# Two blocks of 512 rows as one unit in a two-level Strassen MLP, with six row tiles normalised earlier

## The chip, the cores and the metric

One NeuronCore of a Trainium2 chip runs the whole kernel. The metric is the device time of one execution in microseconds (us). TensorE (PE) does the matmuls, its weight loads are shown as PEld; VectorE is DVE, ScalarE is ACT, GpSimd is POOL, and SyncE (SP) issues the transfers between DRAM and SBUF. All data are FP32.

## The reference

Attention with random features (8 batches, 8 heads, 576 positions, 64 channels, 128 features), then a Fourier mix over positions and channels with a residual, then a normalised two-layer MLP of 512 to 2048 to 512 over 8 x 576 = 4608 rows:

```python
q_p, k_p = phi(q * scale), phi(k * scale)   # phi: exp(x omega^T - |x|^2/2 - max) / sqrt(m)
kv, z = einsum('bhsm,bhsd->bhmd', k_p, v), sum(k_p, axis=2)
x = einsum('bhsm,bhmd->bhsd', q_p, kv) / (einsum('bhsm,bhm->bhs', q_p, z)[..., None] + 1e-06)
...
u = x + real(fft(fft(x, axis=1), axis=2))    # x as (8, 576, 512)
un = (u - mean(u)) / sqrt(var(u) + 1e-06)
out = u + maximum(un @ w_ch1, 0.0) @ w_ch2
```

## The kernel before, in words

**Two parts.** The first part (up to about 423 us in the profile) does the attention of 32 pairs of heads, the Fourier mix (its sums u go to a DRAM tensor `us`), the conversion of the weights, and the MLP of the first 512 rows in four plain tiles of 128 rows. The second part does the MLP of the other 4096 rows in eight blocks of 512 rows (`TB`, `NTB` = 8, numbered j = 0 to 7).

**How a block is computed.** Both layers use Strassen's scheme in Winograd's form (seven products in place of eight), twice nested: a layer is seven outer products (i), each of seven inner ones (n), so 49 "leaves". The order of outer products is `ORDER1` in the first layer and `order(j)` in the second; that of the inner ones is `PARTS` (L1210). A leaf of the first layer (`first_of`, L1495) is four matmuls of 128x128 by 128 rows into one PSUM bank; a leaf of the second (`product_of`, L1892) accumulates four such matmuls into 128 columns. Block 0 does six of its first-layer outer products with one level only (L1646; matmuls of 128 by 256 columns), as the weight sums for two levels are not ready then.

**The operands.** The first layer's weights stay in SBUF (`w1`), with outer sums in `so` (5, 6 and 3), the inner sums of product 1 in `w1s`, and other inner sums in DRAM (`w1l`, three for each of six products, written in block 0 by `w1_inner`). Each block from 1 on loads those 18 (`wx`, L1789, 256 KB each), and every block loads the 49 leaves of the second layer from `w2l` (`wl`, L1798, 256 KB each). Both share one ring of 12 buffers (`wl`, `NWL`). The hidden rows lie in `hid`, four outer cells C11, C12, C21, C22 with four inner cells (f, t) each. The left sums of the second layer (`left_sums`, and `sums` in `product_of`) are added by DVE or POOL (`add`, L1460), as the planner chooses.

**Evictions.** A first-layer leaf's bank is saved or merged by ACT (L1520, L1552) or DVE (L1518, L1538, L1442); a second-layer leaf by ACT (L1865, L1908, L1912, L1934) or DVE (L1870). The second layer's outer sums into the rows u (`ur2`) are L1941 on DVE or POOL; then SP stores the rows (L1006). The last product of all has a shorter end of its own (`ends`, L1806 on).

**The rows.** For blocks 1 to 7 `norm_of` loads a tile of 128 rows (L1067), takes mean and square sum on ACT (L1076, L1081), the factor on POOL (L1085 to L1087), normalises on ACT (L1089) and turns 32x32 blocks on DVE (`by_blocks`, L1024). SP stores the result to DRAM (`turned`, L1032), and `fetched` (L1040) reads it back with the channels on partitions into two `slab` buffers. DVE then makes outer and inner sums of it (`tt`, `unx`, `rx`; L1290, L1257). This is due during the block before, and paced by that block's products.

**The order.** Engines run in the order in which instructions are issued. That order is made when the kernel is built: generators yield `Step`s, each with an engine, a cost, what it waits for and what it takes and gives back, and `Listing.run` picks one at a time. A string names the picks: `PICKS` (1853 steps) in the first part, `PICKS2` (620 steps, two characters each) in the second. Afterwards a model of the engines (`Clock`) and due times choose. `BANKS` and `BANKS2` name PSUM banks in the same way. SP issues nearly all DMAs on one queue, in order.

Of the kernel before, what the change touches and what calls it, by code (L numbers as in the profile page):

```python
# [1 line left out]

# [38 lines left out]
class Clock(NamedTuple):  # L41
# [14 lines left out]
SECOND = Clock(190.0, 0.15, 0.0, 0.1, {}, {}, (PE, ACT, DVE, POOL, SP, NONE), {})  # L56
# [39 lines left out]

PICKS2 = (
    "0w0w0v000u0v0x0y0y0v0y0x0x0v0y0w0z0y0u0t1z0M0u0M1K0K0u1v0Q0N0I0t0W0M0O1L1w0L1U1t0S0Q0R0u010U0S0O0G0G"
    "0P0T1u0R0s0s000S0O0N0N0T0I0P0z0L0Q0R1R0B0K1P0P0K0K0T0V0I0S0G0U0T0S0U1s0H1r0D0z0x0A1N0w0F0S0P0F0E0O1O"
    "1u0R0v0G0V0V0V0C0S1S0R0L0w0P0S1r0V0M0Q0O0u0y0R0H0L1s0U0P0E0F0M0R1r0D0W0M0#0&0u0T0$0W0M0R0J0L0C0O0V00"  # L100
    "0$0N1q0M0R0G0A0V0u0Z0A0A0Z0R0U0D0S0S0L0G0Z0H0P1Y0F0F0Z0Y1q0$0$0C0D0D0U0T0X0T0#0X0z0V0F0U0V0X0C0B0W0P"
    "0R0U0T0U0v0T0x0Y0N1P0z0u0O0z0I0T0M0N0T0K0A0N0R0x0G0W1F0X0L0I0M0I0x0G0T0U0x0R0R0x0G0I0A0R0G0O0O0E0x0M"
    "0V0U000t0E1G1t0T1L0K0B0O0E0P1L0M0u0K0G1Q0L0R1z0N0C0E0G0E0u0G0D0L1D0N0C1Q0K1O0L0S0M0y0C0T0A0B1L0t0U0U"
    "0T0G0L0R0O0E0R0K0O0M0A0J0L0E1r1z1R0z0K0C0y0y0M0O0M1t0I0A0F0D0C0J0I0E1D0L0C0s1K0H0F0J0J0w0z0I0D0E0H1E"
    "0C0J1E0F0p0M0o0L1K1H1N0M0B0O0G0C0F0J0A0J0J0N0p1G0C1B0H0N0y0E0E0I1H0y1K0G0z0B0L0H0G0N1H0M0H0M0M0M0M1E"
    "0C1J0G0B1I0B1E0y0G0u1E0F0B0D1D1E0u0F0F0y0A0z0y0G0C0J0A0p0D0G0y1G0C0F0z0p0E0u1w0A0D1w0y0y0x0z0F0t0E0B"
    "0F0E1x1v1z1D0C0A0E0E0C0z0t1z0D0C0D1C0B0D0u0x0B0r0x0C0v0A1y0v0u0v0t0t0A0u0o0s0z0A1x0y0C0z0y0A0x0D0A0t"
    "0D0E0E0E0D0A0z0y0z0B0q0s0C0A0x1r0x0z0z1t1D1D0t0s0u0v0r0t0v000u0u0q0r0A1A0x0z0A0s0z0A1q0z0x0y0A0p0v0u"
    "0x0p0p0z0x0x0y0t0w0y0r0q0v0r0q000n0t0E0r0r0n0E0F0A0A0A0G0z0F0p0x0z0L0L0x0z0y0x0H0J0o0w0G0C0G0m0x0v0E"
    "0w0z0A0v0B0x0F0G0A0D0B0I0z0z0G0C0m0E0x0y"  # L110
)
BANKS2 = (
    "5670152675637645127567567560754361752071640532471365062476735"
# [39 lines left out]
def picked(text, n):  # L153

    if n == 1:
        return [divmod(DIGITS.index(c), 36) for c in text]
    return [(int(text[i]), DIGITS.index(text[i + 1])) for i in range(0, len(text), n)]


class Listing:  # L160
# [72 lines left out]
    def run(self, streams, picks=(), banks=""):  # L233
        todo = []
        picks = iter(picks)
# [18 lines left out]
        while todo:  # L254
# [44 lines left out]
            go_on(item)  # L299

# [32 lines left out]
def kernel(  # L333
# [10 lines left out]
    nc = tc.nc  # L344
# [42 lines left out]
    w1 = const.tile([128, NDC, DFF], F32, name="w1")  # L387
# [632 lines left out]

    def by_blocks(j, i, pool, u, h, k):
        yield Step(DVE, 0.69, take=("turn",), give=("u",), makes=("turn", j, i))
        w = pool.tile([P, 4, NDC, Q], F32, name="turn", tag="turn", bufs=1)
        nc.vector.transpose(  # L1024
            out=w[:].rearrange("p g d q -> p d g q"),
            in_=u[:].rearrange("p (d g q) -> p d g q", d=NDC, g=4),
        )
        if (j, h) not in turned:
            turned[j, h] = dram.tile([P, 4, 2, NDC * Q], F32, name=f"turned{j}_{h}")
        t = turned[j, h]  # L1030
        yield Step(SP, 0.55, 6.0, after=(("turn", j, i),), makes=("turned", j, i), give=("turn",), kb=165)
        nc.sync.dma_start(t[:, :, k], w[:].rearrange("p g d q -> p g (d q)"))  # L1032

    def fetched(j, h, dst):
        yield Step(
            SP, 1.7, 3.0, after=(("turned", j, 2 * h), ("turned", j, 2 * h + 1)),
            makes=("unT", j, h), kb=330,
        )
        for g in range(4):
            nc.sync.dma_start(  # L1040
                dst[Q * g : Q * g + Q].rearrange("q (b k) d t -> q b (k d t)", k=2),
                turned[j, h][:, g].rearrange("(b q) k n -> q b (k n)", q=Q),
            )

    def normed(j, pool):
        t0 = (NPLAIN * TP + TB * j) // 128

        def paced(i):
            h, k = divmod(i, HT // 128)
            yield Step(  # L1050
                NONE,
                after=events_of(range(t0, t0 + TB // 128)) + ((("first", j - 1, (1, 1, 5, 2)[i]), "y"),),
            )
            yield from norm_of(
                j, t0 + 2 * h, i, pool, None, (h, k), ((("first", j - 1, (6, 2, 7, 3)[i]), "y"),)
            )

        for i in range(TB // 128):
            yield Fork(paced(i), LEAF * (98 * j - 60 + 8 * i))

    def norm_of(j, t, i, pool, dst, block=None, after=()):

        yield Step(SP, 0.42, 3.0, take=("u",), kb=256)
# [134 lines left out]
    def rest(t, b, yp):  # L1198
# [6 lines left out]
        store_rows(t, ur[:])  # L1205

# [18 lines left out]

    def single(j):
# [12 lines left out]
    def tokens(j, i, n):  # L1239

        whole = outer_tokens(j, i)
        if n in (1, 2, 3, 7):
            t, d = {1: (0, 0), 2: (0, 1), 3: (1, 1), 7: (1, 0)}[n]
            return whole[:, 4 * t : 4 * t + 4, d]
        return extra_of(j, i)[:, (5, 6, 4).index(n)]

    def extra_of(j, i):
        if i == 1:
# [10 lines left out]
    def token_sums(j):  # L1259
        if j == 1:  # L1260
            yield Step(NONE, after=tuple(("w1l", i, n) for i in twice(1) for n in (5, 6, 3)))
        for i in twice(j):
            for m, op in enumerate(inner_tokens(j, i)):
                yield Step(
                    DVE, 0.28, after=(("tt", j),), makes=("tokens", j, i) if m == 3 else None, port=True,
# [4 lines left out]
    def block_norms(j, pool):  # L1270
        t0 = (NPLAIN * TP + TB * j) // 128
        yield Step(NONE, take=("slab",) * 4, after=events_of(range(t0, t0 + TB // 128)) + ("converted",))
# [36 lines left out]


# [63 lines left out]
    GW = F2 // 2  # L1374
    w1s = const.tile([128, 4, GW], F32, name="w1s")

# [7 lines left out]
    def weights_of(j, i, n):  # L1384
# [21 lines left out]
    def pairs(start):  # L1406
        for n in range(start, B * NP, NS):
            yield from attn(n)

    every = mybir.EngineType  # L1410
# [9 lines left out]
        BANKS,  # L1420
    )
# [13 lines left out]
        slab=0, u=2, turn=1, ur=3, s=6, sq=5, set=3, wl=NWL, sums=NSUM, part=4,  # L1435
    ).items()}
    hid = late.tile([128, 4, 2, 2, 4 * P], F32, name="hid")
    so.update({i: late.tile([128, D2, F2], F32, name=f"so{i}") for i in (5, 6, 3)})
# [7 lines left out]
    def cell_of(c, f, t):  # L1446
        return hid[:, c, f, t]
# [7 lines left out]
    def add(o, l, r, op, engines=(POOL, DVE), **kw):  # L1455
        n = math.prod(o.shape[1:]) / 512
        step = Step({e: {POOL: 1.3, DVE: 0.65}[e] * n + 0.05 for e in engines}, port=True, **kw)
# [8 lines left out]
    def first_of(j, i):  # L1466
        me = ("first", j, i)
        slot, read = slot_of(j, i), READ.get(i)
        free = ((("second", j - 1, read), "read"),) if read and j else ()
        merged, final = i in WITH, i in (2, 3, 4)  # L1470
# [3 lines left out]
        def over(f, t):  # L1474

            if i == 2:
                return (("h", j, 6, f, t),) if j else ()
            return {7: (("h", j, "u4", f, t),), 4: (("h", j, "sum", f, t),)}.get(i, ())

        def leaf(n, ps, start, after=(), take=(), give=(), makes=None):  # L1480
            own = n in (5, 6, 3) and i != 1
            w = ("wx", 1) if i == 1 else ("wx", j, i, n) if own else ("so", i, n)
            token = (("tokens", j, i),) if i != 1 else (("tt", j),)
            yield Step(
                PE, 0.895, after=token + (w,) + after, take=take, give=(("wl",) if own else ()) + give,
# [7 lines left out]
            left, right = weights_of(j, i, n), tokens(j, i, n)  # L1493
            for f in range(4):
                nc.tensor.matmul(  # L1495
                    ps[:, P * f : P * f + P].rearrange("f (b q) -> f b q", q=Q),
# [8 lines left out]
        def made(f, t):  # L1505
            return ("h", j, i, f, t)

        def with_(f, t):
            return (("h", j, BEFORE[i], f, t),)
# [31 lines left out]
        def moved(f, t, ps, give, name):  # L1541
# [8 lines left out]
            else:  # L1550
                yield Step(ACT, 0.6, 0.1, after=free, give=give, makes=(me, name), bias=AT[name])
# [519 lines left out]
```

## Time and profile before

| | us |
|---|---|
| runs | 1132.73, 1135.31, 1133.30; median 1133.3 |
| the profiled execution, device time | 1134.51 |
| its span, first to last instruction | 1132.7 |
| first part, up to the first leaf of block 0's L1495 in the chain | 423.3 |
| second part, from there to the last matmul's end | 705.8 |
| after the last matmul | 3.6 |

The granted TensorE clock is 1.000. The transfers amount to 258.3 MB, 228 GB/s over the span. The groups that hold most time are:

```profile
L1892 PE MATMUL banks<-wl,sums 128*128 128x128 f32 x1792 | 218.9, 275 | 0.7 <-DVE sums L1460 0.7
L1892 PE MATMUL banks<-wl,hid 128*128 128x128 f32 x1344 | 170.6, 275 | 0.6 <-DVE part L1870 0.4
L618 ACT ACTIVATE e<-banks,nmx 128x128 f32<-128x128 f32 x576 | 164.3, 423 | 24.3 <-DVE nmx L601 23.7
L1495 PE MATMUL banks<-rx,wx 128*128 128x128 f32 x672 | 88.8, 275 | 0.0
...
wl<-w2l SPq DMA_DIRECT2D x392, 256.0 KB
wx<-w1l SPq DMA_DIRECT2D x126, 256.0 KB
```

A group's line names the code line, the engine, the operation, what it writes and reads, the shape and the count; then its busy time, the mean duration of one in ns, and the engine's idle time just before, with what ended it. Matmuls overlap in their pipeline, so 275 ns is longer than the distance from one to the next. The last two lines are DMA issues with the size of each.

### The profile page before, as it was taken

The page shows a single profiled execution, that of the slowest core. Times are in us where ns is not written, and L with a number is a line of the kernel's source. Part 1 is how long each engine was busy: PE and PEld are TensorE (multiplying, and loading weights), DVE is VectorE, ACT ScalarE, POOL GpSimd, SP SyncE. Part 2 cuts the span into 40 slices and gives each one's busy share as a digit, 9 for nine tenths or more (in the row PEclk, how much of TensorE's full clock was granted, in tenths as well). Part 3 has the DMA queues.
Part 4 walks back from the last instruction along what each step waited for, and adds up shares of the span by engine and source line. Part 5 has one row for each costly group of instructions (what it writes and reads, how often), then busy time and mean ns, then how long its engine had stood idle before and what let it go on. Part 6 is the DMA issues. An engine that isn't in the chain of part 4 may idle for free.

```text
span 1132.7 us, 34265 instructions
## 1 busy us (share of the span) xinstructions
PE 1116.3 (99%) x13643; PEld 1040.2 (92%) x13643; DVE 867.6 (77%) x1732; ACT 541.7 (48%) x1644; POOL 428.1 (38%) x438
## 2 busy tenths in 40 slices
PE   8999999999999999999999999999999999999998
PEld 7778888879868778999999999999999999999998
DVE  6999899987576655796787778678678678678666
ACT  7888898856535216614424424424423522522311
POOL 2443443654573214613612710710720630540361
PEclk9999999999999999999999999999999999999999
DMA  7856766565763238797797798797698698798576
GB/s 242 224 177 180 224 181 215 170 206 170 222 196 126 93 92 284 211 314 246 227 339 232 219 329 241 213 326 258 202 323 264 210 281 298 214 268 293 184 223 205
DMA packets 187966, 258.30 MB, mean 228 GB/s; under 512 B 52384, under 2 KB 83360, under 8 KB 187808
## 3 DMA queue, kind: packets, MB, share of 16 engines
q1 hardware_dynamic: 187312, 255.85, 73.1%
q8 instruction: 109, 1.79, 0.7%
q14 instruction: 49, 0.40, 0.1%
q10 hardware_dynamic: 496, 0.26, 0.1%
HBM read 212.27 MB, written 47.97 MB: 230 GB/s over the span
## 4 chain that ended last, share of the span: by engine, by line
PE 89%; DVE 4%; ACT 3%; DMA 2%; issue 1%; SPq 0%; DVEq 0%; ACTq 0%
PE banks L1892 28%; PE banks L1495 28%; PE banks L1167 5%; PE banks L658 5%; PE banks L1190 5%; PE banks L564 4%; PE banks L1646 4%; PE banks L692 3%; PE banks L739 2%; PE banks L901 2%; ACT e L618 1%; PE banks L851 1%; DMA unT<-turned 1%; DVE nmx L601 1%; PE banks L861 1%
## 5 line engine op out<-in xcount | busy, mean ns | idle before, releaser
L1892 PE MATMUL banks<-wl,sums 128*128 128x128 f32 x1792 | 218.9, 275 | 0.7 <-DVE sums L1460 0.7
L1892 PEld LDWEIGHTS banks<-wl,sums 128*128 128x128 f32 x1792 | 209.3, 192 | 1.1 <-DVE sums L1460 0.9
L618 ACT ACTIVATE e<-banks,nmx 128x128 f32<-128x128 f32 x576 | 164.3, 423 | 24.3 <-DVE nmx L601 23.7
L1460 POOL TENSOR_TENSOR hid<-hid 128x512 f32<-128x512 f32 x97 | 127.0, 1314 | 119.1 <-ACT hid L1552 66.5
L1892 PE MATMUL banks<-wl,hid 128*128 128x128 f32 x1344 | 170.6, 275 | 0.6 <-DVE part L1870 0.4
L1892 PEld LDWEIGHTS banks<-wl,hid 128*128 128x128 f32 x1344 | 160.2, 192 | 1.1 <-DVE part L1870 0.6
L601 DVE TENSOR_REDUCE nmx<-banks 128x8 f32<-128x1024 f32 (+1 forms) x96 | 89.4, 952 | 18.3 <-PE banks L658 14.2
L1495 PE MATMUL banks<-rx,wx 128*128 128x128 f32 x672 | 88.8, 275 | 0.0
L1865 ACT ACTIVATE s<-banks 128x128 f32<-128x128 f32 x112 | 30.8, 277 | 113.2 <-PE banks L1892 97.7
L1495 PEld LDWEIGHTS banks<-rx,wx 128*128 128x128 f32 x672 | 81.8, 192 | 0.0
L658 PE MATMUL banks<-om,kqT 64*64 64x128 f32 (+1 forms) x2088 | 78.7, 275 | 2.2 <-ACT kv L708 1.9
L1538 DVE TENSOR_TENSOR hid<-banks,s 128x512 f32<-128x512 f32 x72 | 49.7, 691 | 38.9 <-PE banks L1495 36.9
L658 PEld LDWEIGHTS banks<-om,kqT 64*64 64x64 f32 (+1 forms) x2088 | 64.3, 138 | 13.1 <-issue 3.6
L1870 DVE TENSOR_TENSOR part<-banks,s 128x128 f32<-128x128 f32 x112 | 32.1, 288 | 50.0 <-PE banks L1892 48.8
L1520 ACT ACTIVATE s<-banks 128x512 f32<-128x512 f32 x65 | 38.7, 596 | 59.7 <-PE banks L1495 58.6
L1167 PE MATMUL banks<-unT,w 128*128 128x128 f32 x512 | 65.4, 279 | 1.7 <-DVE qeT L578 1.7
L507 POOL TENSOR_TENSOR w<-w,raw 128x512 f32<-128x512 f32 x28 | 37.7, 1356 | 77.6 <-DVE raw L501 77.6
L1442 DVE CUSTOM_DVE_ANT_0 hid<-banks,s 128x512 f32<-128x512 f32 x63 | 43.6, 692 | 27.5 <-PE banks L1495 25.2
L1167 PEld LDWEIGHTS banks<-unT,w 128*128 128x128 f32 x512 | 60.2, 192 | 4.5 <-issue 2.3
L1460 DVE TENSOR_TENSOR hid<-hid 128x512 f32<-128x512 f32 x91 | 61.1, 712 | 3.8 <-ACT hid L1598 3.8
L1518 DVE TENSOR_TENSOR s<-banks,hid 128x512 f32<-128x512 f32 x70 | 48.4, 691 | 19.0 <-PE banks L1495 16.7
L1941 POOL TENSOR_TENSOR ur<-ur,part 128x512 f32<-128x512 f32 x21 | 26.8, 1281 | 95.4 <-ACT part L1934 91.6
(200 smaller groups left out, 2387.4 us busy)
## 6 DMA issues: line engine op xcount, KB each, us to landing
wl<-w2l SPq DMA_DIRECT2D x392, 256.0 KB
wx<-w1l SPq DMA_DIRECT2D x126, 256.0 KB
raw<-in_moe_w_ch_dram SPq DMA_DIRECT2D x32, 512.0 KB
kq<-in_k_dram SPq DMA_DIRECT2D x32, 288.0 KB
kq<-in_q_dram SPq DMA_DIRECT2D x32, 288.0 KB
vd<-in_v_dram SPq DMA_DIRECT2D x32, 288.0 KB
u<-us SPq DMA_DIRECT2D x36, 256.0 KB
ur<-us SPq DMA_DIRECT2D x36, 256.0 KB
```

The lines of the kernel that those rows point to most:

```text
L564: nc.tensor.transpose(ps[:, (j - j0) * 128 : (j - j0 + 1) * 128], src(j), ident[:])
L601: nc.vector.tensor_reduce(nmx[:, :, 0:num], pps[:, :, 0 : MF * num].rearrange("p b (c m) -> p b c m", m=MF), axis=AX.X, op=ALU.max, negate ...
L618: nc.scalar.activation(out=e[:, c + (i if num == 1 else 0), :], in_=pps[:, i, MF * c : MF * c + MF], func=AF.Exp, bias=nmx[:, i, c : c + 1],)
L658: nc.tensor.matmul(pps[cols, c, MF * m : MF * m + MF], lhsT=kqT[rows, j, cols], rhs=om2[rows, :],)
L1167: nc.tensor.matmul(hp[:, 0:TP], lhsT=w1[:, dc, 128 * fc : 128 * fc + 128], rhs=unTs[key][:, dc, :], start=(dc == 0), stop=(dc == NDC - 1),)
L1190: nc.tensor.matmul(yp[:, 0:DM], lhsT=hs[fc][:, 128 * i : 128 * i + 128], rhs=w2[:, fc, :], start=(fc == 0), stop=(fc == NFC - 1),)
L1460: eng.tensor_tensor(out=o, in0=l, in1=r, op=op)
L1495: nc.tensor.matmul(ps[:, P * f : P * f + P].rearrange("f (b q) -> f b q", q=Q), lhsT=left[:, P * f : P * f + P], rhs=right, start=start an ...
L1518: nc.vector.tensor_tensor(out=s[:], in0=ps, in1=cell_of(addend, f, t), op=ALU.add)
L1538: nc.vector.tensor_tensor(out=o, in0=ps, in1=kept[saved][:], op=ALU.add)
L1646: nc.tensor.matmul(cell.rearrange("f t (b q) -> f t b q", q=Q), lhsT=w[:, d, col : col + 128], rhs=right[:, :, d].rearrange("f (t b) q -> ...
L1892: nc.tensor.matmul(ps[:, 0:128], lhsT=left[:, f], rhs=wls[j, i, n][:, f], start=start and f == 0, stop=(f == 3), skip_group_check=True,)
```

## The change

**Blocks 2 and 3, 4 and 5, 6 and 7 form a unit each** (`WIDE`, `wide`, `head`, `unit`). In the first layer of a unit a leaf takes the rows of both blocks: it is two matmuls of 128x128 by 256 rows, and covers half of the product's hidden columns; so each outer product runs twice (g = 0, 1 in `passes`) with the same tokens. The number of leaves and of evictions stays (98 in a unit for two times 49). All 49 weight leaves of the first layer are now written to DRAM (`w1x`), and a unit loads them in 49 tiles of two half leaves (the first unit takes product 1 from SBUF and loads 42). In the second layer both blocks use a `wl` tile before it is given back; their products alternate, and the second block's leaf n waits for the first's.

```diff
+            for m in range(7):
+                after = tuple(("w1x", i, PARTS[k % 7]) for k in (2 * m, 2 * m + 1))
+                yield Step(SP, 0.45, 2.6, take=("wl",), after=after, kb=165, makes=("wx", j, i, m), ...
...
-            for f in range(4):
+            left, right = weights_of(j, i, n, g), tokens(j, i, n)
+            for f in range(4 * P // span):
                 nc.tensor.matmul(
-                    ps[:, P * f : P * f + P].rearrange("f (b q) -> f b q", q=Q),
+                    ps[:, span * f : span * f + span].rearrange("f (b q) -> f b q", q=Q),
...
+            shared = ((("second", j - 1, i), {5: "p5 read", 4: "read"}.get(n, n)),) if j != head(j) else ()
...
-                give=("wl",) + give,
+                give=(() if wide(j) and j == head(j) else ("wl",)) + give,
```

**Where it lies.** A unit's hidden rows need twice the place: C11 and C12 lie where `hid` was, C21 and C22 on the place of `w1`, once nobody reads that (`moved`). The rows of a unit lie on the places of `so` 5 and 6, the additional row buffers and sums on that of `so` 3, and part of the token sums on `w1s`.

```diff
+    def moved():
+        yield Step(
+            NONE,
+            after=tuple(("w1x", i, n) for i in ORDER1 for n in PARTS)
+            + tuple((("first", WIDE, 1, g), "leaves") for g in range(2)),
+            makes="moved",
+        )
+        spread(const.tile([128, 4 * DFF], F32, name="hx", tag="w1")[:])
```

`first_of` adds `("moved",)` to what the second product of block 2 waits for, and the whole of block 1's last read of `hid` to what the first unit's evictions wait for.

**Weights to DRAM.** Nine raw weight leaves are stored in the first part, behind the output stores of the plain tiles 0, 1 and 2 (four, four and one). Of the others, 18 are stored in block 0 as before; 22 are new in the second part (`w1_stored`): 12 in block 0, six in block 1's first layer, four from `w1s` at the start of the first unit.

```diff
         store_rows(t, ur[:])
+        for i, n in RAW[4 * t : 4 * t + 4] if t < 3 else ():
+            nc.sync.dma_start(leaf_in(i, n), weights_of(0, i, n))
...
+    def w1_stored():
+        for k, (i, n) in enumerate((i, n) for i in (6, 5, 7, 3) for n in (1, 2, 4)):
+            after = tuple(("sum", i, d, f) for d in range(2) for f in range(2))
+            yield from w1_store(i, n, after, LEAF * (20 + 2 * k))
+        for k, i in enumerate(INNER):
+            yield from w1_store(i, 7, (("so", i, 7), (("first", 1, ORDER1[k], 0), "y")), LEAF * (102 + 7 * k))
+        for n in (5, 6, 3, 7):
+            yield from w1_store(1, n, ((("first", WIDE, 1, 0), "y"),), LEAF * 196)
```

**Six tiles earlier.** The four row tiles of block 1 and the first two of block 2 (`EARLY`) are normalised and turned in the first part, in a buffer that held q and k (`ahead`). Their instructions, of the same kinds as those of `norm_of`, are put between the steps of the first part after the step numbers in `BETWEEN` (from step 1662 on, up to 1846); `PICKS` and `BANKS` of that part stay.

```diff
+            placed += 1
+            while between and between[0][0] == placed:
+                next(between.pop(0)[1], None)
```

**The rest.** In the units the fetch of the turned rows is eight DMAs where it was four, and the token sums have 256 columns. The left sums of the last unit are on DVE alone. The order of the last unit's products is that of the last block before. `PICKS2` has 1105 steps of three characters, `BANKS2` 102 banks. The planner's model has a transfer rate of 240 where it had 190, and other costs for a wide leaf (0.866) and for DVE's additions in units (0.55).

More of the change, by code (lines that the diff above doesn't have):

```diff
@@ L1 @@
 from contextlib import ExitStack
+from functools import partial
 import math
@@ L55 @@
 )
-SECOND = Clock(190.0, 0.15, 0.0, 0.1, {}, {}, (PE, ACT, DVE, POOL, SP, NONE), {})
+SECOND = Clock(240.0, 0.15, 0.0, 0.1, {}, {}, (PE, ACT, DVE, POOL, SP, NONE), {})
 SLACK, AHEAD = 0.3, 4.0
@@ L1019, with turned_of @@
     turned = {}
+    def turned_of(j, h):
+        if (j, h) not in turned:
+            turned[j, h] = dram.tile([P, 4, 2, NDC * Q], F32, name=f"turned{j}_{h}")
+        return turned[j, h]
     def by_blocks(j, i, pool, u, h, k):
-        yield Step(DVE, 0.69, take=("turn",), give=("u",), makes=("turn", j, i))
-        w = pool.tile([P, 4, NDC, Q], F32, name="turn", tag="turn", bufs=1)
+        more = j > WIDE + 1 and i % 2
+        held = "turnx" if more else "turn"
+        free = *((("first", WIDE, 1, g), "leaves") for g in range(2)), *(("w1x", 1, n) for n in PARTS)
+        yield Step(DVE, 0.69, take=(held,), give=("u",), after=free if more else (), makes=("turn", j, i))
+        if more:
+            w = w1s[:].rearrange("p n f -> p (n f)")[:, 1536:2048].rearrange("p (g d q) -> p g d q", g=4, d=NDC)
+        else:
+            w = pool.tile([P, 4, NDC, Q], F32, name="turn", tag="turn", bufs=1)[:]
@@ L1420 @@
         BANKS,
+        betweens(),
     )
```

431 lines of the change are left out of this document (324 added, 107 removed).

## The prediction

> **What bounds the kernel now.** I read the engine totals first, then the chain that ended last, then busy time by 20 us stretches, then the order of time where a stretch was not full.
>
> ```profile
> PE 1116.3 (99%) x13643; PEld 1040.2 (92%) x13643; DVE 867.6 (77%) x1732; ACT 541.7 (48%) x1644; POOL 428.1 (38%) x438
> ...
> PE 89%; DVE 4%; ACT 3%; DMA 2%; issue 1%; SPq 0%; DVEq 0%; ACTq 0%
> ```
>
> TensorE holds 89% of the chain; no other engine has more than 4%. Where it is not full is the next question.
>
> ```profile
> 460.00:480.00 20.00, 20.00 (x137) 18.79 (x137) 16.03 (x22) 13.65 (x32) 12.07 (x13) 1.00 0.74 220
> 480.00:500.00 20.00, 20.00 (x181) 20.00 (x180) 18.92 (x31) 3.98 (x16) 4.00 (x3) 1.00 1.04 300
> 500.00:520.00 20.00, 19.27 (x173) 19.08 (x172) 14.95 (x38) 5.35 (x17) 1.68 (x2) 1.00 0.96 334
> ...
> 760.00:780.00 20.00, 20.00 (x182) 20.00 (x181) 18.46 (x44) 5.30 (x16) 0.00 (x0) 1.00 0.89 290
> ```
>
> Columns: PE, PEld, DVE, ACT, POOL busy, granted clock, DMA share, GB/s. The second part (from 423.34 us on) is full but for 0.73 us in 500-520, 0.22 us in 920-940 and 0.39 us at the end. Counting gives the same: with the durations below, 742 leaves (block 0: 7 + 49, blocks 1 to 7: 98 each) and 192 rows of L1646 make 662.9 + 41.5 = 704.4 us, and with the three gaps 705.8: just what lies between 423.34 and the last matmul's end at 1129.14. So this part gets shorter only by fewer or cheaper matmuls. Busy marks can overlap, so I take durations from start to start:
>
> ```profile
> 454.44 1.89 PE L1646 MATMUL banks<-unT,w 128*128 128x256 f32 x8
> 456.17 1.89 PE L1646 MATMUL banks<-unT,so 128*128 128x256 f32 x8
> ...
> 619.26 1.06 PE L1495 MATMUL banks<-unT,w 128*128 128x128 f32 x8
> 620.15 1.06 PE L1495 MATMUL banks<-tt,so 128*128 128x128 f32 x8
> 621.05 1.06 PE L1495 MATMUL banks<-rx,wx 128*128 128x128 f32 x8
> 621.94 0.72 PE L1495 MATMUL banks<-unT,w 128*128 128x128 f32 x5
> ```
>
> Each FP32 matmul leaves two rows. A 128x128 row takes 2.68 us / 24 = 111.7 ns, so a leaf (four matmuls, eight rows) 0.893 us. For 128x256 the chain has 152 rows in 32.81 us: 215.9 ns.
>
> **The change part by part, against the span of 1132.7 us.** The profiled execution is given as 1134.51 us and the runs' median as 1133.3, so I add 0.6 to the span at the end.
>
> 1. First-layer leaves of blocks 2 to 7: six blocks x 49 = 294. Each has been four 128x128 matmuls (8 x 111.7 = 893 ns) and becomes two of 128x256 (4 x 215.9 = 863 ns): 30 ns x 294 = **-8.8 us**. The wide row is taken from block 0, whose operands are strided alike; the ends are the rounding of the eight-row starts (1.725 to 1.73 us), -8.5 to -8.9. Second-layer leaves stay at 893 ns and in number. The Trainium skill ("TensorE: Matmul & The Clock Gate", "Wait — 56ns, not 53.3ns?") puts a warm matmul at N / 2.4 GHz plus about 2.5 ns; with two passes to a row that gives 111.7 ns, as the trace has, but 218.3 ns for 256 columns, and a saving of 20 ns x 294 = 5.9 us. The trace's 215.9 ns speaks against it, so the term stays.
>
> 2. Block 1's start. The one stall of the second part's beginning:
>
> ```profile
> 502.43 0.69 DVE L1290 TENSOR_TENSOR tt<-unT,unT 128x512 f32<-128x512 f32 x1 [0.92 <-DMA unT<-turned]
> ...
> 508.39 1.16 PE L1892 MATMUL banks<-wl,sums 128*128 128x128 f32 x8 [0.73 <-DVE sums L1460]
> ```
>
> DVE got the fetched rows late, did block 1's sums in a rush, and PE waited for a left sum queued behind them. With block 1's four tiles normalised in the first part, the fetch needs only the slabs: **-0.7** (0 if something else is late there).
>
> 3. The six tiles in the first part. Each issues two 256 KB DMAs on SP (load, store), three ACTIVATEs (622 + 720 + 806 ns by L1076, L1081, L1089), three small POOL operations (241 + 594 + 197 ns) and one transpose on DVE (703 ns): ACT 12.9 us in all, POOL 6.2, DVE 4.2. They stand late in the order, behind the last pairs' exponentials (which end at 365 us), and ACT has room there:
>
> ```profile
> 372.84 0.38 ACT L945 ACTIVATE bmp<-banks 64x258 f32<-64x258 f32 x1 [7.25 <-PE banks L912]
> ...
> 388.68 0.28 ACT L1153 ACTIVATE ht<-banks 128x128 f32<-128x128 f32 x1 [5.82 <-PE banks L1167]
> ...
> 423.16 0.58 ACT L1527 ACTIVATE banks<-banks 128x512 f32<-128x512 f32 x1 [15.68 <-PE banks L1495]
> ```
>
> Those three gaps alone are 28.8 us. Without them each tile would hold ACT 2.1 us in front of an eviction, and a full PSUM bank stops PE. The new wait is ACT's on the load: queued behind it are the evictions L1153 and L874. L1076 waited at most 2.3 us for its load; three tiles with no gap to hide it make 6.9. Also in the first part, nine 256 KB stores of raw first-layer weights go behind the plain tiles' output stores (303, 347 and 389 us), four DMAs at 303 ahead of a q load on SP: at 0.4 us each 1.6 us later. DMA share there is 0.77. POOL's small operations stand among the second layer's weight sums (L1332), where it sat idle 17.70 us in one piece up to 365.04; what queues behind them there are L962 and L963. Taken: **+0.7**, bounds 0 and +7; nearer 0, since PE's rows are gapless from 340 to 423.
>
> 4. Transfers in the second part. Added: 22 stores of weights (12 + 6 + 4) x 256 KB = 5.8 MB in blocks 0 and 1 and at the first unit's start. Gone from there: two of the eight tiles normalised, 1.0 MB; come in: block 3's fetch, 1 MB. From 420 to 600 us the stretches moved 47.4 MB; 53.2 MB in 180 us is 295 GB/s, while 500-520 reached 334. It fits, with a tenth to spare, if it goes where there is room (440-480, 520-560). If none fits, 5.8 MB / 334 GB/s = 17.3 us late. Taken **+0.5**, bounds 0 and +17.3. Later the load falls: a unit needs 49 + 49 weight tiles where two blocks took 134, so its wait becomes rarer; no gain, as nothing waits there now.
>
> 5. Start of the first unit. Half its hidden cells lie on w1's place, so the evictions of its second product wait for the last four w1s stores, issued after leaf 3 (2.7 us). They land some 4 x 0.9 us of transfer and 2 to 5 us later (a weight load took 5.12 us in the chain), 8 to 11 us; the first eviction into that place follows leaf 17, 15 us. Behind that eviction on DVE stand the next products' evictions, and for their banks waits PE. **0**, bounds 0 and +5. SP's weight loads queue behind such waits, with 12 buffers ahead (20 us of leaves in a unit).
>
> 6. Sums. Unit token sums are 24 of 256 columns in place of 48 of 128 (285 ns; by 285 and 691 ns about 420): DVE -3.6 us a unit, under PE, so 0. If DVE were the bound (18.46 of 20 in 760-780) it would be a small gain. Fetches double in number, 16 more SP issues of about 0.43 us a unit, also under PE: 0.
>
> 7. The end. Block 6 now finishes half a product before block 7, and its last 512 KB store (0.81 us of issue for two, like 1127.82 in the order of time) stands on SP before block 7's. **+0.5**, bounds -0.4 (the end's gap gone) and +2.5.
>
> Sum: -8.8 - 0.7 + 0.7 + 0.5 + 0 + 0 + 0.5 = -7.8; span 1124.9, runs **1125.5 us**. Own range 1122.8 to 1129.
>
> **The rivals.**
>
> A. Half the gain is given back: the transfer wait of point 4 costs 4 to 5 us around 500-520 and 580-605, where the share is 0.95 or more already. For it: the 0.73 us stall lay in just such a stretch. Against: the stretches before have room. 1125.5 + 4.5 = 1130.
>
> B. No change: the two-block order leaves gaps of its own, at the one boundary where block 1's products can't be mixed with the next (its cells are shared), and at unit starts. Three boundaries at some 2.5 us (a seed, an eviction and a sum, 0.6 + 0.6 + 0.7, plus hops) and the transfer wait: 1125.5 + 7.5 = 1133. Against: within a unit each product is followed by its twin, so a dependence has 14 leaves (12 us) where it had 7.
>
> C. Slower: SP works strictly in order, so a weight store that waits for its sum holds every load behind it, and wl's 12 buffers (10.7 us of leaves while blocks are single) run dry in blocks 0 and 1. Price: the stores' whole 17.3 us on PE: 1125.5 - 0.5 + 17.3 = 1142. It decides for slower once more than 7.8 + 2.3 us beyond my sum is lost. Against: SP waited at most 5.0 us at a time there (for the transpose).
>
> D. The wide matmul costs as much for a column as the narrow one: -8.8 falls away, 1134. The rows of L1646 speak against it.
>
> **How the numbers follow.** A measurement of this kernel can tell 0.2%, 2.3 us, from no change. Forecast 0.66; A 0.12; B 0.08; C 0.12; D 0.02. Faster: forecast and A, 0.78. Same: most of B and part of D, 0.09. Slower: C and the rest, 0.13. The range takes in A and most of B: 1122.8 to 1133.3; below it would need the whole saving and none of the costs.
>
> **What would show it.** Right: 1176 rows of 128x256 at the first-layer leaf's line in the second part, starts 1.73 us apart for eight; no PE idle of 0.73 near block 1's start; the second part near 697 us from its first leaf. Weight loads fall from 518 tiles to 403. Point 3 is wrong if PE shows gaps in 300-423 ended by ACT evictions or kq loads; point 4, if wl or unT transfers end PE's waits in 480-610; point 5, if PE stands some 12 us after the first unit's start. The prediction falls if the second part is not full, or the wide rows are not near 216 ns.

## The result, and the profile after

| | before | after |
|---|---|---|
| runs, median us (lowest to highest) | 1134.01 (1131.69 to 1137.93), 22 runs | 1130.19 (1124.67 to 1134.22), 22 runs |
| the profiled execution, device time | 1134.51 | 1128.43 |
| its span | 1132.7 | 1126.6 |
| first matmul of block 0's first-layer leaves | 422.06 | 421.52 |
| from there to the last matmul's end | 707.1 | 701.5 |
| after the last matmul | 3.6 | 3.6 |

Ratio 0.9963, 95% interval 0.9952 to 0.9974: 4.2 us faster (2.9 to 5.4; 3.8 by the medians), where 7.8 were forecast. Two more series of the kernel after, `again` and `third`, gave 0.9973 and 0.9974. The second part is measured here from the first of block 0's leaves, 1.3 us ahead of the point that the prediction used, so the forecast's second part is 707.1 - 8.8 - 0.7 + 0.5 + 0.5 = 698.6, and without any wait of its own (707.1 less the three gaps of 1.34 and the 8.8) it would be 697.0.

The totals and the chain's shares, from the page of the kernel after:

```profile
PE 1108.2 (98%) x12467; PEld 1000.7 (89%) x12467; DVE 888.1 (79%) x1705; ACT 541.8 (48%) x1644; POOL 357.4 (32%) x381
...
PE 90%; DMA 3%; DVE 3%; ACT 2%; SPq 1%; issue 0%; DVEq 0%; ACTq 0%
```

TensorE is still the bound, with 8.1 us less of busy time, but DMA and DVE hold some more of the chain. Where TensorE isn't full, by stretches of the kernel after (columns as before):

```profile
480.00:500.00 20.00, 19.57 (x171) 19.03 (x170) 17.84 (x25) 6.83 (x24) 8.52 (x8) 1.00 1.04 312
500.00:520.00 20.00, 18.66 (x164) 18.47 (x165) 16.45 (x37) 7.38 (x21) 8.08 (x10) 1.00 0.92 279
560.00:580.00 20.00, 20.00 (x179) 19.89 (x179) 16.87 (x32) 3.26 (x13) 0.00 (x0) 1.00 0.97 303
580.00:600.00 20.00, 18.61 (x160) 18.16 (x159) 16.52 (x33) 4.02 (x16) 0.00 (x0) 1.00 1.00 358
...
660.00:1110.00 450.00, 450.00 (x3169) 426.11 (x3168) 357.90 (x627) 142.72 (x366) 95.18 (x100) 1.00 0.65 195
```

The three units are gapless in this profile: 450.00 of 450 us (449.06 in `again` and 449.72 in `third`, one short wait each). Apart from 0.39 us at the very end, all that is lost in the second part lies in the second layers of the single blocks, 1.77 us in 480 to 520 (block 0) and 1.39 us in 580 to 600 (block 1). What ended these waits, from the list of TensorE's waits after 423 us (total, times, longest) and from the order of time:

```profile
PE banks L2153 <- DMA wl<-w2l: 1.8, 3, 0.8
PE banks L2153 <- DVE part L2129: 1.8, 3, 0.9
```

```profile
486.04 1.16 PE L2153 MATMUL banks<-wl,hid 128*128 128x128 f32 x8 [0.37 <-DMA wl<-w2l]
500.90 1.16 PE L2153 MATMUL banks<-wl,hid 128*128 128x128 f32 x8 [0.93 <-DVE part L2129]
502.50 2.05 PE L2153 MATMUL banks<-wl,hid 128*128 128x128 f32 x16 [0.44 <-DVE part L2129]
581.33 1.13 PE L2153 MATMUL banks<-wl,hid 128*128 128x128 f32 x8 [0.60 <-DMA wl<-w2l]
585.10 1.16 PE L2153 MATMUL banks<-wl,hid 128*128 128x128 f32 x8 [0.79 <-DMA wl<-w2l]
```

Half of it is weight tiles that came late. The other half is an eviction (L2129) that came late; at 500 it stood behind sums of block 1's rows on DVE, and the 0.39 us at the end are of this kind too. That the rows are late again is seen on SP, in the order of time of the kernel after: the fetch of block 1's second half stands behind 17 weight loads, and DVE gets it at 497.6:

```profile
470.78 1.95 SPq L1091 DMA_DIRECT2D unT<-turned  x4
473.19 15.25 SPq L2049 DMA_DIRECT2D wl<-w2l  x17
488.49 1.89 SPq L1091 DMA_DIRECT2D unT<-turned  x4
```

The waits come to 3.5 us with the last one of 0.39 us. The second part is 4.5 us above 697.0. By an estimate the rest is the pipeline filling again: a matmul takes 275 ns where its successor follows after 111.7, so each of the six breaks would cost some 0.16 us beside its idle time. No run shows this apart.

### The profile page after: what moved, and what is told of

It reads as the page before. It is cut to its first block, busy times and chain, and to the rows that moved or that the text cites. A ratio compares the mean times of both kernels' runs of the same rounds, so it can differ in the third digit from the quotient of the medians.

```text
span 1126.6 us, 31534 instructions
## 1 busy us (share of the span) xinstructions
PE 1108.2 (98%) x12467; PEld 1000.7 (89%) x12467; DVE 888.1 (79%) x1705; ACT 541.8 (48%) x1644; POOL 357.4 (32%) x381
## 4 chain that ended last, share of the span: by engine, by line
PE 90%; DMA 3%; DVE 3%; ACT 2%; SPq 1%; issue 0%; DVEq 0%; ACTq 0%
PE banks L2153 30%; PE banks L1710 27%; PE banks L690 5%; PE banks L1235 5%; PE banks L596 5%; PE banks L1258 5%; PE banks L1861 4%; PE banks L724 3%; PE banks L771 2%; PE banks L933 2%; PE banks L883 1%; DMA wl<-w2l 1%; DMA kq<-in_q_dram 1%; PE banks L893 1%; ACT e L650 1%; PE banks L944 1%
## 5 line engine op out<-in xcount | busy, mean ns | idle before, releaser
L2153 PE MATMUL banks<-wl,hid 128*128 128x128 f32 x768 | 99.2, 276 | 3.1 <-DMA wl<-w2l 1.8
L2153 PEld LDWEIGHTS banks<-wl,hid 128*128 128x128 f32 x768 | 92.6, 192 | 4.5 <-DVE part L2129 1.8
L1710 PE MATMUL banks<-unw,wxw 128*128 128x256 f32 x352 | 85.5, 379 | 0.0
L2153 PE MATMUL banks<-wl,hx 128*128 128x128 f32 x576 | 74.2, 275 | 0.4 <-DVE part L2129 0.4
L1710 PEld LDWEIGHTS banks<-unw,wxw 128*128 128x128 f32 x352 | 66.6, 190 | 8.9
L1710 PE MATMUL banks<-rx,wxw 128*128 128x256 f32 x288 | 71.2, 379 | 0.0
L1710 PE MATMUL banks<-ttw,wxw 128*128 128x256 f32 x288 | 70.0, 379 | 0.0
L2153 PEld LDWEIGHTS banks<-wl,hx 128*128 128x128 f32 x576 | 69.4, 192 | 0.7 <-DVE part L2129 0.6
L1710 PEld LDWEIGHTS banks<-rx,wxw 128*128 128x128 f32 x288 | 54.5, 190 | 7.3
L1258 PE MATMUL banks<-w,ht 128*128 128x512 f32 x128 | 58.8, 598 | 0.0
```

The lines of the kernel that those rows point to most:

```text
L1258: nc.tensor.matmul(yp[:, 0:DM], lhsT=hs[fc][:, 128 * i : 128 * i + 128], rhs=w2[:, fc, :], start=(fc == 0), stop=(fc == NFC - 1),)
L1710: nc.tensor.matmul(ps[:, span * f : span * f + span].rearrange("f (b q) -> f b q", q=Q), lhsT=left[:, P * f : P * f + P], rhs=right, start ...
L2153: nc.tensor.matmul(ps[:, 0:128], lhsT=left[:, f], rhs=wls[head(j), i, n][:, f], start=start and f == 0, stop=(f == 3), skip_group_check=True,)
```

## The experiments

All runs, beside the kernel before on the same chip. "Second part" is from the profiled execution, from block 0's first leaf to the last matmul's end; the last two columns are TensorE's busy time in two stretches of 40 us.

| kernel | median us (runs) | ratio to before, 95% | second part | 470-510 | 560-600 |
|---|---|---|---|---|---|
| before | 1134.01 (22) | 1 | 707.1 | 39.27 | 40.00 |
| after | 1130.19 (22) | 0.9963, 0.9952 to 0.9974 | 701.5 | 38.23 | 38.61 |
| again | 1129.15 (12) | 0.9973, 0.9957 to 0.9989 | 701.7 | 38.83 | 38.25 |
| third | 1130.00 (12) | 0.9974, 0.9958 to 0.9990 | 702.1 | 38.03 | 38.48 |
| narrow | 1137.60 (9) | 1.0038, 1.0024 to 1.0052 | 711.5 | 37.88 | 38.11 |
| twice | 1131.59 (12) | 0.9982, 0.9967 to 0.9997 | 703.0 | 38.45 | 38.34 |
| quiet | 1133.85 (12) | 0.9995, 0.9979 to 1.0012 | 705.3 | 38.44 | 36.67 |
| first_part | 1134.29 (12) | 1.0002, 0.9987 to 1.0016 | 707.8 | 38.83 | 40.00 |
| half | 1123.63 (6) | 0.9915, 0.9899 to 0.9932 | 697.7 | 39.27 | 40.00 |
| nofetch | 1125.51 (6) | 0.9931, 0.9912 to 0.9949 | 699.1 | 38.28 | 40.00 |
| tiny | 1128.97 (12) | 0.9959, 0.9943 to 0.9975 | 700.7 | 38.53 | 38.83 |
| actall | 1154.30 (5) | 1.0171, 1.0147 to 1.0195 | 728.3 | 33.88 | 30.95 |
| early12 | 1134.56 (12) | 1.0008, 0.9992 to 1.0024 | 698.1 | 39.35 | 40.00 |
| hoist | 1136.99 (12) | 1.0029, 1.0014 to 1.0043 | 701.7 | 39.35 | 38.26 |
| hoist2 | 1135.88 (12) | 1.0021, 1.0007 to 1.0035 | 699.8 | 39.35 | 39.46 |
| placed12 | 1137.71 (6) | 1.0051, 1.0038 to 1.0064 | 700.8 | 39.44 | 40.00 |
| placed8 | 1129.78 (6) | 0.9972, 0.9960 to 0.9983 | 701.6 | 39.35 | 37.06 |

### Do the wide matmuls pay? (narrow)

Each matmul of 256 columns becomes two of 128, with all else as after:

```diff
-                nc.tensor.matmul(
-                    ps[:, span * f : span * f + span].rearrange("f (b q) -> f b q", q=Q),
+                for h in range(span // P):
+                    at, nb = span * f + P * h, P // Q
+                    nc.tensor.matmul(
+                        ps[:, at : at + P].rearrange("f (b q) -> f b q", q=Q),
...
```

Expected:

> The changed kernel with each 128x256 matmul of a unit's first layer split into two of 128x128, all else in place. Theory 'transfers' (the missing 4 us are PE's waits for weights and rows in blocks 0 and 1, added stores are the cause): 294 leaves x 30 ns = +8.8 us on the changed kernel, about 1139 us. Theory 'first part' (early tiles and raw stores slow the first part): +8.8 as well. If the wide matmuls bring less in place than the row of block 0 says, +4 to +6.

Measured: 711.5 us of second part, 9.4 to 10 more than after; by the two ratios the runs are 8.5 us slower, where 8.8 was expected. The chain of waits shows the same first layer of a unit in narrow and in after:

```profile
610.34 81.29 PE banks L1712 x728
```

```profile
610.22 78.57 PE banks L1710 x364
```

78.57 / 364 = 215.9 ns for a wide row, 81.29 / 728 = 111.7 ns for a narrow one: 7.5 ns a row, and three units of 392 rows make the 8.8 us of the forecast. Rival D falls. The Trainium skill ("TensorE: Matmul & The Clock Gate", "Wait — 56ns, not 53.3ns?") has a formula by which, as an estimate with two passes to a row, a wide row would take 218.3 ns; the measured 215.9 decides.

### Does the first part pay? (first_part)

The kernel before gets the six early tiles and the nine raw stores, all into spare tensors:

```diff
+            while between and between[0][0] == placed:
+                next(between.pop(0)[1], None)
...
+        for i, n in RAW[4 * t : 4 * t + 4] if t < 3 else ():
+            nc.sync.dma_start(w1x[i][PARTS.index(n)], weights_of(0, i, n))
```

Expected:

> The kernel before, with the six early tiles and the nine raw weight stores added to its first part in their places, their results left in spare tensors; its second part stays whole. 'First part': +2 to +4 us against the kernel before. 'Transfers' and 'order': 0 to +0.7, the first leaf of block 0 at 423 to 424 us.

Measured: 1.0002 (0.9987 to 1.0016), and block 0's first leaf at 419.57. The six tiles and the nine stores cost nothing that the runs show where they stand. That leaf starts anywhere from 418.9 to 422.0 in the profiles of kernels with the same first part, so a difference of 2 us in one profile's start says nothing.

### The 22 added weight stores (twice, quiet)

In `twice` each of the 22 new stores of the second part is issued a second time, into a spare tensor. In `quiet` they are moved into the first part:

```diff
+        nc.sync.dma_start(again[i][PARTS.index(n)], w)
```

```diff
+        for i, n in MOVED[0:14] if t == 1 else MOVED[14:] if t == 2 else ():
+            nc.sync.dma_start(leaf_in(i, n), weights_of(0, 1, 1))
...
-        w = weights_of(0, i, n)
-        nc.sync.dma_start(leaf_in(i, n), w)
```

Expected:

> The changed kernel with the 22 weight stores of the second part issued twice, the second time to a spare tensor: 5.8 MB or 17.3 us of transfer at 334 GB/s more. 'Transfers': blocks 0 and 1 already move some 295 GB/s, so much of it becomes wait, +5 to +15 us. 'First part': 0 to +1. 'Order' (the two-block order has gaps of its own, without transfers): 0 to +1.

> The changed kernel with the 22 weight stores of the second part left out there and issued behind the output stores of plain tiles 1 and 2 in the first part, with raw weights in place of the sums; the output is not the reference's. 'Transfers' by the added stores: -3 to -5 us, about 1126, and no wait of PE for weights in blocks 0 and 1. 'First part' and 'order': 0, or some slower by the additional stores in the first part.

Measured: with another 22 stores the second part is 703.0 us, 0.9 to 1.5 more than in the three profiles of the kernel after; the runs (0.9982 against 0.9963 to 0.9974, with intervals that overlap) can't tell it from nothing. Taking the stores away brought nothing either: 0.9995. If they were the cause, 5.8 MB more should cost about as much as the 4 us that are missing, and 5.8 MB less should bring them back. Rival C, which put the whole price on these stores, falls with it. `quiet` is even slower than after. TensorE's waits in its second part are 5.2 us in place of 3.6, and why its weight tiles come later still isn't shown; the other part is the clock. Its stretch, and a piece of its chain; then the same piece in placed8, which waited 1.82 us at that place:

```profile
580.00:600.00 20.00, 17.43 (x136) 16.76 (x135) 12.71 (x25) 2.87 (x12) 0.00 (x0) 0.91 0.93 302
```

```profile
590.35 13.43 PE banks L2155 x104
```

```profile
584.67 12.77 PE banks L2177 x112
```

129 ns a row with the granted clock at 0.91, 114 ns with the clock at 1.00. The loss sits in the first 16 rows of that piece: they take 3.44 us from start to start in `quiet`, where 16 rows take 1.79 at 111.7 ns. The wait before it was 1.77 us; the piece costs 1.8 us more than its 104 rows at 111.7 ns.

### Supply in blocks 0 and 1 (half, nofetch, tiny)

`half` loads 128 KB for each second-layer weight tile of blocks 0 and 1, and the matmuls read that half twice. `nofetch` leaves out the 32 fetches of the first unit's rows (POOL fills the place). `tiny` is nofetch with 32 transfers of 2 KB, DRAM to DRAM, in the places of the fetches on SP, so that the issues stay and the bytes go.

```diff
+                    n = 256 if j < WIDE else 512
+                    nc.sync.dma_start(wl[:].rearrange("p f m -> p (f m)")[:, 0:n], w2l[i][STORED.index(l)][:, 0:n])
```

```diff
-                for t in range(2):
+                if j <= WIDE + 1 and not g:
+                    nc.gpsimd.memset(dst, 0.01)
+                for t in range(2 if j > WIDE + 1 else 0):
```

```diff
+                for t in range(0 if j > WIDE + 1 else 2):
+                    tiny = dram.tile([Q, 16], F32, name=f"tiny{j}_{h}_{g}_{t}")
+                    nc.sync.dma_start(tiny[:], turned[j, h][0:Q, g, t, 0:16])
```

Expected:

> The changed kernel, where the second-layer weight tiles of blocks 0 and 1 are loaded only by half (128 KB in place of 256 KB), and their matmuls use the loaded half twice; PE's work is the same, the output is not the reference's. 'Supply' (PE's waits in 470 to 510 and 560 to 600 us come from the weight loads of the single blocks' second layers, 293 GB/s, meeting the fetches of rows): the gaps go, -3 to -5 us on the changed kernel, about 1126. 'Order' (the new order of the engines makes them, whatever the transfers take): -1 to 0.

> The changed kernel with the 32 fetch DMAs of the first unit's rows (2 MB, 541 to 584 us) left out; four memsets on POOL fill the place, so the output is not the reference's. 'Fetch' (the second stretch, 560 to 600 us, is late because 32 more issues stand on SP between the weight loads): that stretch is full, -2 to -3 us on the changed kernel, and the first stretch stays as it is. 'Supply': -1, as 2 of some 16 MB in that stretch go. 'Order': 0.

> Like the kernel without the first unit's fetch, but with 32 very small DMAs (32 rows of 64 bytes, DRAM to DRAM) at the places of the 32 fetch DMAs on SP; the output is not the reference's. 'Issue' (the fetch costs by the 0.43 us that SP needs for each): as the changed kernel, ratio 0.997, and gaps in 560 to 600 us. 'Bytes' (it costs by its 2 MB in a stretch where the transfers are full): as without the fetch, ratio 0.993, and that stretch full.

Measured: `half` takes the whole loss away, but for 0.73 us in 470 to 510 that the kernel before loses as well. 697.7 us is within 0.7 of the second part without waits; the runs gain 5.5 us on `again`, a little more than the 3 to 5 expected, and the six of them lie within 1.9 us (1123.29 to 1125.18) where 46 runs of the kernel after span 11.2. `nofetch` frees 560 to 600 (40.00 of 40) and leaves 470 to 510 as it was (38.28): the first unit's fetch is issued from 541 on. The clearest view is SP's own waits between 560 and 590, in before, after, half, nofetch and tiny in this order (total us, times, longest):

```profile
SPq L1798 <- PE banks L1892: 7.7, 19, 0.5
SPq L1798 <- DMA wl<-w2l: 1.8, 4, 0.6
SPq L1798 <- DMA unT<-turned: 1.2, 3, 0.6
```

```profile
SPq L2049 <- DMA wl<-w2l: 3.1, 8, 0.8
SPq L1086 <- DMA wl<-w2l: 2.6, 6, 1.0
SPq L2049 <- PE banks L2153: 1.7, 6, 0.4
```

```profile
SPq L2050 <- PE banks L2154: 6.6, 15, 1.1
```

```profile
SPq L2051 <- PE banks L2155: 16.4, 30, 1.4
```

```profile
SPq L2054 <- DMA wl<-w2l: 3.5, 11, 0.7
SPq L2054 <- PE banks L2158: 3.4, 8, 1.2
```

Where SP's loads wait for PE, the ring of 12 buffers is full and TensorE sets the pace. That is so before the change (7.7 against 3.0), in half and in nofetch. In the kernel after it is the other way round (1.7 against 5.7; with all lines of these views, 3.5 against 8.0 in `again` and 3.7 against 8.3 in `third`): SP waits for earlier transfers, the loads run behind, and TensorE waits for them in the end. The first stretch tells the same by SP's waits between 470 and 500: 7.6 for PE against 4.0 for earlier transfers before the change, 5.5 against 9.9 after it, 4.1 of these in one wait that ended with the load of a row tile. In `placed8` below, which moves the transfers of two row tiles away from there, it is 11.8 against 0.4.

With the issues but hardly any bytes (`tiny`) SP is between the two, TensorE has 38.83 us of 40, and the second part is 700.7. So of the 2.4 to 3.0 us between the three profiles of the kernel after and nofetch the issues seem to hold 1.6 (700.7 against 699.1); that is one profile each, the small DMAs hold SP longer than the fetches that they replace (median 564 ns against 424), and the runs (0.9959 against 0.9963 to 0.9974) can't tell tiny from after. The split between bytes and issues stays open; that leaving out the fetches takes away more than half of the loss doesn't.

### Another queue for the fetches (actall)

All fetches are issued by ACT in place of SP:

```diff
-                    nc.sync.dma_start(
+                    nc.scalar.dma_start(
```

Expected:

> The changed kernel with every fetch of turned rows issued on ACT's queue in place of SP's, at the same places in the order; the bytes are the same. 'Fetch' by SP's issue time (0.43 us each, 104 DMAs) and by the weight loads queued behind their waits: -2 to -3 us. 'Supply': 0. Against it: ACT's evictions queue behind 0.4 us issues and behind a wait for a row that is not turned, +1 to +3.

Measured: 1154.30, 24 us slower than after, far outside both expectations (-2 to -3, and +1 to +3). Two lines of actall, the largest group of TensorE's waits and one of ACT's evictions:

```profile
PE banks L2153 <- ACT banks L2169: 10.8, 5, 3.2
```

```profile
592.23 0.26 ACT L2169 ACTIVATE banks<-banks 128x128 f32<-128x128 f32 x1 [5.81 <-DMA unw<-turned]
```

An issue that waits for transfers ahead of it holds everything behind it on its engine. On SP that is loads with a ring in front of them; on ACT it is evictions, and TensorE waits for them. The granted clock is 0.91 in both stretches as well, so not all of the 24 us is waiting.

### More tiles in the first part (early12, hoist, hoist2, placed8, placed12)

If the rows' traffic is what doesn't fit, more of it can go where TensorE has room. `early12` normalises all twelve tiles of blocks 1 to 3 in the first part. `hoist` adds to that the first unit's 32 fetches in one go, meant for 541 to 556 (548 to 568 in its profile), and `hoist2` both halves of block 1's fetch together.

```diff
-    EARLY = [(j, i) for j in (1, 2) for i in range(TB // 128)][:6]
+    EARLY = [(j, i) for j in (1, 2, 3) for i in range(TB // 128)]
```

```diff
+                if j <= WIDE + 1:
+                    for _ in range(4):
+                        if hoisted:
+                            next(hoisted[0], None)
+                    continue
...
+            for hh in (h, 1 - h) if j not in both else ():
```

Expected:

> The changed kernel with all twelve tiles of blocks 1 to 3 normalised in the first part; the order of all other instructions stays. It takes 6 x 512 KB = 3.1 MB of transfers, 12 ACT and 6 DVE instructions out of 460 to 570 us. 'Supply': -1 to -2 us on the changed kernel, ratio 0.995 to 0.996, as the fetch stays in the full stretch. 'First part' (room ends at six tiles): +1 to +3.

> The kernel with twelve early tiles, and the first unit's 32 fetch DMAs issued in 541 to 556 us in place of 541 to 584 us. 'Supply': the full stretch 560 to 600 us loses 0.9 MB more, -2 to -3 us on the changed kernel, ratio 0.994 to 0.995, and no wait of PE for weights there. 'Issue': the burst on SP delays the weight loads behind it, 0 to +2.

> The same, and also both halves of block 1's rows fetched at once near 471 us, where the second half stood behind 17 weight loads (488 us). If the rest of the loss is DVE waiting for that half while PE's evictions queue behind: -0.5 to -1.5 us on the former, ratio 0.993 to 0.994. If the weight loads behind it are what PE needs first: 0 to +2.

Measured: in early12 the second part is 698.1 us, 3.4 under after and 0.5 under the forecast's 698.6, and its two stretches are as full as before the change. But the whole is 1134.56, as the first leaf of block 0 comes at 430.36, 8.8 us later than after; -1 to -2 us was expected of 'supply' and +1 to +3 of 'first part'. TensorE's two waits in the first part of early12, by the order of time:

```profile
394.07 0.63 PE L1182 MATMUL banks<-ident,u 128*128 128x128 f32 x4 [2.83 <-DVE u L1178]
...
411.64 1.09 PE L1182 MATMUL banks<-ident,u 128*128 128x128 f32 x4 [3.96 <-DVE u L1178]
```

The rows of block 0 (`u`) come late, as their loads and their small operations on POOL queue behind those of the additional tiles. The waits are 6.8 us; the granted clock of 0.83 in 400 to 420 goes with them. Fetching earlier gains nothing: the second part grows again by 3.6 us in hoist and 1.7 in hoist2. Of that 1.7 and 0.5 are waits for weight tiles, so the burst has only moved; 1.0 in each is a wait that early12 doesn't have, for an eviction on DVE near the end of the first unit's first layer (695 to 697 us).

`placed12` puts the six tiles elsewhere: stores behind block 0's loads, POOL's operations away from block 0's, three tiles in other buffers. `placed8` moves only the two tiles of block 2 that the change had left.

```diff
+        if (j, i) in EARLY[9:]:
+            place = att.tile([128, R, 128], F32, name="kqT", tag="turned")[:].rearrange("p r c -> p (r c)")
```

Expected, with the third series of the kernel after beside them:

> All twelve tiles of blocks 1 to 3 normalised in the first part, as in early12, but the six additional ones put where that trace shows the engines idle: stores behind the plain tile's loads on SP, POOL's small operations away from the plain tiles' factors, three tiles in buffers that held q and k transposed. Theory S (the loss of 4.5 us sits in blocks 0 and 1 of the second part, where the weight loads leave no room for the rows' loads and stores; early12 lost its gain only by 6.8 us of PE waits at 391 and 408 in the first part): second part 698 us as in early12, first leaf of block 0 at 419 to 422, so about 3.5 us under the kernel after, 1126 to 1127, ratio 0.993 to 0.995. Rival F (the first part has no room for 12 tiles wherever they stand): first leaf at 425 or later, time 1131 or more. Rival N (early12's short second part is only the late start, with more loads done before it): second part 701 again, time as after.

> Only the two other tiles of block 2 are moved into the first part, at the same places. Theory S: these two tiles' loads and stores (four DMAs of 256 KB) leave the stretch from 470 to 510; about a third of the waits goes: second part 700, time 1 to 1.5 us under the kernel after. Rival F: nothing gained, first leaf late by 1 us or more. Rival N: 0.

> The kernel after once more, beside the two: second part 701.5 to 703, ratio 0.997, about 1129 to 1130.

Measured: placed12 is slower still. One load of block 0's rows, issued behind the three additional ones, leaves DVE without work for 9.8 us, and TensorE waits 8.4 us for it:

```profile
394.44 0.69 DVE L1172 BATCH_NORM_STATS2 st<-u 128x6 f32<-128x512 f32 x1 [9.80 <-DMA u<-us]
```

Its second part, 700.8 where theory S asked for 698, loses nothing more in the two stretches than early12, but 1.5 us at 438 (block 0's first layer, an eviction on ACT) and 1.0 at 696. So theory F holds at these two placings: the first part takes six tiles for nothing, but with twelve the first leaf comes 7 to 9 us later. `placed8` has no such cost (first leaf at 421.16) and fills 470 to 510 (39.35 against 38.03 to 38.83), and loses it again at 560 to 600 (37.06), so the time is that of the kernel after, where 1 to 1.5 us less was expected. Its first stretch is full without a late start, which speaks against rival N there. Whether the late start of the kernels with twelve tiles helps their second stretch isn't shown; their second part lies 7 to 9 us later, so that the fixed stretches cover somewhat other work. No version was found that is faster than it and computes the same.

## Why the prediction was right in direction and wrong in size

**The count.** 742 leaves and 192 rows make 704.4 us, but the first of these leaves starts at 422.06, ahead of the point 423.34 up to which the sum was compared. That it came out as "just what lies between" was luck; some 1.3 us of the second part before are in no term, and the differences below don't hang on them.

**Step 1, wide leaves, -8.8:** right, by row (215.9 ns) and by experiment (`narrow`). Its ends are a little narrow: starts of 1.725 to 1.73 us give some -8.3 to -9.1.

**Step 2, block 1's start, -0.7:** wrong. "With block 1's four tiles normalised in the first part, the fetch needs only the slabs": true, but it still stands in SP's order between the weight loads, and came at 497.6 where it came at 502.4 before. The stretch 470 to 510 lost 0.73 us before and 1.2 to 2.0 in three profiles after.

**Step 3, early tiles, +0.7:** it was 0 (`first_part`). Its upper bound of 7, made of ACT's waits for loads, is close to what twelve tiles cost (`early12`: 6.8 us of waits), but by chance: there TensorE waited for block 0's rows.

**Step 4, transfers in the second part, +0.5:** this is the step that failed. It took a mean over 180 us (295 GB/s; 282 were moved) and concluded "It fits, with a tenth to spare, if it goes where there is room". The loads can't go there: 12 buffers are 10.7 us of leaves, so what matters is each stretch of some ten microseconds in which single blocks take 256 KB every 0.893 us, 293 GB/s, before any row is fetched. There the second part lost 2.9 to 3.5 us more than the forecast's 698.6: steps 2 and 4 together were put at -0.2 us, and with step 1 as measured they come to +3.2 to +3.8 in the three profiles. With half the bytes in the weight tiles it is gone (`half`, 697.7). The place is rival A's, around 500 to 520 and 580 to 605; A's price of 4.5 us is somewhat high for it, and that its 1130 meets the median of 1130.19 is partly luck, as the sum below shows. The step also named the wrong transfers: the 22 stores weigh some 1.5 us or less (`twice`), the fetches and row tiles more (`nofetch`, `placed8` in the first stretch).

**Step 5, the first unit's start, 0:** right; 600 to 660 has no gap in the three profiles of the kernel after. **Step 6:** right for the sums, wrong for "Fetches double in number, 16 more SP issues of about 0.43 us a unit, also under PE: 0". The first unit's fetches are issued among the single blocks' weight loads, and there their issues alone seem to cost TensorE 1.2 us in 560 to 600 (`tiny` against `nofetch`). **Step 7, the end, +0.5:** 0; 3.56 us after the last matmul in both.

**The sum.** The profiled execution's span fell by 6.1 us (1132.7 to 1126.6): the second part is 2.9 us above the forecast, and the first part 1.2 below it (no cost in place of 0.7, and a start 0.5 earlier, which is within its scatter). The medians fell by only 3.8, since the profiled execution after is 1.8 us faster than its median and the one before 0.5 slower. So 1.7 of the 4 us that are missing are seen in this pair of profiles, and 2.3 are differences between runs of one kernel; the last section has what is known of them.

Rival B put losses at the units' boundaries, where the profile after has none. C's mechanism (a store that waits for its sum holds SP) was hardly seen for the 22 new stores: at their line SP waited 2.5 us in all from 423 to 640, 0.6 of it for a sum and the rest for other transfers. At the 18 old ones it waited 5.3 us for sums, where it was 4.1 before.

## What to carry to other kernels

Ask of a load queue who ends its waits. If it is the consumer, through buffers coming free, the ring is ahead; if it is the queue's own earlier transfers, it is behind, and the next addition will be paid by the engine that sets the time, though that engine still shows 98% busy. And judge added transfers over a stretch as long as the ring lasts, not over the part's mean. When work is moved into a part with idle engines, look at the loads whose order it changes: six tiles there were free, and eight as well, twelve cost more than the whole change brought.

## What the hardware showed that was not expected

The granted clock fell after short waits in one profile. In `quiet` a wait of 1.77 us, with 0.51 and 0.17 in the 7 us before, was followed by 0.91 in that stretch; in placed8 waits of 1.12 and 1.82 us within 5 us were not. The Trainium skill ("TensorE: Matmul & The Clock Gate", "What's actually happening") says that the clock falls after an idle window of about 3.4 us; here it fell, in one profile, with less than 2.5 us of waits in 7. After the 8.4 us of placed12 the clock is low too, as that rule has it: 0.85 in 380 to 400.

Of 46 runs of the kernel after, 24 with a mean clock of 0.999 or 1.000 average 1128.6 us, and 22 below that 1131.7. Of the 101 runs of the kernel before that the experiments have beside them, only 19 are below 0.999; they average 1135.9, the other 82 1133.2. The shorter kernels `half` and `nofetch` have none below 0.999 in 12 runs. So by these shares an estimate of some 1 us of the 4 goes with the clock (22 of 46 times 3.1, less 19 of 101 times 2.7). That the short waits lower it is argued from this, not shown; what each run lost the traces of single profiles can't show.
